# Linear attention and a gated feed-forward layer on one core: the sums over keys in two column halves of the TensorE array

## The chip, the cores and the metric

The kernel runs on one core of one Trainium2 chip. A core has TensorE (PE, matrix products), VectorE (DVE), ScalarE (ACT), GpSimd (POOL) and SyncE (SP, which issues the DMAs here). The metric is the device time of one execution in microseconds (us). A product on PE has a stationary operand, which is loaded into the array first (a weight load, PEld in the profile), and a moving operand, which is streamed through it; the result goes to partitions of a PSUM bank, one partition for each stationary column.

## The reference

For 8 batches and 8 heads of 576 tokens with 64 numbers each, attention is computed with feature maps in place of a softmax. The output of all heads then goes through a gated feed-forward layer (4608 tokens, 512 to 1536 to 512).

```python
def phi(x):
    proj = np.einsum('bhsd,df->bhsf', x, w_phi)          # 64 -> 128
    proj = proj - np.max(np.abs(proj), axis=-1, keepdims=True)
    return np.concatenate([np.exp(proj), np.exp(-proj)], axis=-1)   # 256 features
q_p, k_p = (phi(q), phi(k))
kv = np.einsum('bhsf,bhsd->bhfd', k_p, v)
z = np.sum(k_p, axis=2)
num = np.einsum('bhsf,bhfd->bhsd', q_p, kv)
den = np.einsum('bhsf,bhf->bhs', q_p, z)[..., None] + 1e-06
x = num / den                      # then, over all tokens and heads:
out = (silu(x @ w_gate) * (x @ w_val)) @ w_out
```

The part in question is `kv` and `z`: sums over the 576 keys of a head.

## The kernel before, in words

Two heads are handled together as a pair; there are 32 pairs. For a pair, the keys come in five tiles of 128 tokens (the last holds the remaining 64 tokens of both heads), in three groups: two tiles, two tiles, and the last one (`GROUPS`). For each group PE projects the keys (128 tokens to 128 features for each head), DVE finds the largest absolute value of each token and head (L449) and subtracts it (L454, the centring), ACT takes the two exponentials (L458, L459), and PE multiplies the 128 features of each sign, as stationary operand, by the values (64 numbers and two ones, so that the sum `z` comes along) as moving operand. These last products are the sums over keys. The function `values` issues them: L474 for the four full tiles, once for each tile, head and sign (16 products of 66 columns in a pair), and L467 for the last tile, once for each sign (2 products of 132 columns, both heads at once). They accumulate in one bank, `ps_kv`, whose 128 partitions are the 128 features. All operands here are float32. When the last tile is in, ACT copies the sums out (L495), and they are the stationary operand of the numerators and denominators of the queries.

The queries of the first 8 pairs are handled as the keys are; for the other 24, their largest values are found with DVE's 32 by 32 transposes (L573), a reduction (`largest`, L581), a merge over groups of partitions (`over_groups`, L584 to L589) and another transpose (L593).

The feed-forward layer runs on tiles of 384 tokens, with each float32 number split in a high and a low part and three products for one; from about 720 us on it runs alone, in another form (`pair`, L1008).

The order on every engine is made when the program is built. Each piece of work is a step with an engine, an estimated cost, a rank and the steps it comes after; a small simulation of the engines (`Plan.run`) starts, on each free engine, the ready step with the lowest rank, and writes the instructions in that order. The sums are one step for each group, with the cost `2 * n * pe32(D2)`. On the chip each engine works through its own list, and semaphores hold it where an operand isn't ready. Where PE has no ready step, the plan puts in a product with zeros (L1092 to L1096).

Of the kernel before, what the change touches and what calls it, by code (L numbers as in the profile page):

```python
# [17 lines left out]
P = 128  # L18
S = 576
# [14 lines left out]
D2 = D + 2  # L34
# [30 lines left out]
class Plan:  # L65
# [16 lines left out]
    def add(self, eng, cost, fn, after=(), rank=0.0, take=None, give=None):  # L82
        s = Step(eng, cost, fn, rank, len(self.steps), self.LAG[eng], take, give, (rank, len(self.steps)))
        seen = set()
        for a in after:
            if a is not None and id(a) not in seen:
                seen.add(id(a))
                a.then.append(s)
                s.left += 1
        s.early = self.early  # L90
        self.steps.append(s)
        return s
# [79 lines left out]
def dve(n):  # L172
    return 150 + 1.04 * n
# [10 lines left out]
def act(n):  # L184
    return 190 + 0.86 * n


def pe(n):
    return max(58, 7 + 0.441 * n)


def pe32(n):
    return 2 * max(112, 0.85 * n)
# [3 lines left out]
def favor_attention_moe(ctx: ExitStack, tc: tile.TileContext, qT, kT, v, w_phi, wg, wv, wo, out):  # L197
    nc = tc.nc
# [44 lines left out]
    def view(tag, shape, dtype=F32, when=0, o=None):  # L243
        n = size(shape)
        if o is None:
            o = filled.get((tag, when), 0)
            filled[tag, when] = o + n
        assert o + n <= ROOM[tag], (tag, when, o + n)
        made = lambda: shaped(space(tag, when, F32 if dtype is U32 else dtype)[:, o:o + n], shape, dtype)
        return made if when else made()  # L250

    get = lambda x: x() if callable(x) else x
# [6 lines left out]
    vf = [view("m2", [5, 2, D2])] * 2  # L259
# [16 lines left out]
    def bank(name):  # L276
        return banks.tile([P, 512], F32, name=name, tag=name)
# [3 lines left out]
    ps_kv = bank("kv")  # L281
# [26 lines left out]
    add = plan.add  # L308

    def matmuls(terms):  # L310

        for o, l, r, a, z in terms:
            nc.tensor.matmul(o, l, r, start=a, stop=z)  # L313
# [56 lines left out]
    last = {}  # L370

    def attention(i, rank):
# [4 lines left out]
        one = 0 if early else j  # L377
# [3 lines left out]
        rk, rq, rm, rn, rt = (rank + (0 if early else o) for o in OFFSETS)  # L381
# [22 lines left out]
        n = 4 * P * P  # L404
# [19 lines left out]
        for g, (t0, t1) in enumerate(GROUPS):  # L424

            tail = t1 == 5
            w = t1 - t0
            n = 1 if tail else 2 * w
            key = ("k", i, g)
            buf = (3 * i + g) % 2  # L430
            view = lambda key=key, n=n: work[plan.bank[key]][:, :n * NF].rearrange("p (n f) -> p n f", f=NF)
            room = kp[buf].rearrange("p t h s f -> p (t h) s f")[:, :n]

            def project(t0=t0, t1=t1, key=key, tail=tail):
                o = work[plan.bank[key]]
                for t in range(t0, t1):
                    c = slice(t * P, (t + 1) * P)
                    acc = o[:, :NF] if tail else o[:, (t - t0) * 256:(t - t0 + 1) * 256]
                    if plain:
                        matmuls([(acc, get(kin[one])[:, c], wst if tail else wbd, True, True)])  # L440
                    else:
                        khi, klo = (ks()[:, n, c] for n in range(2))
                        w_hi, w_lo = (wst_hi, wst_lo) if tail else (wbd_hi, wbd_lo)
                        matmuls([(acc, khi, w_hi, True, False), (acc, khi, w_lo, False, False), (acc, klo, w_hi, False, True)])

            width = NF if tail else 256
            kproj = add("PE", w * (pe32(width) if plain else 3 * pe(width)), project, k_ready, rk, take=key)
            m = km[(3 * i + g) % len(km)][:, :n]
            kmax = add("DVE", dve(n * NF), lambda m=m, view=view: vec.tensor_reduce(  # L449
                out=m, in_=view(), axis=AX.X, op=ALU.max, apply_absolute_value=True),  # L450
                       [kproj, last.get(("km", 3 * i + g - 4))], freeing)

            def centre(n=n, m=m, view=view, room=room):
                vec.tensor_tensor(out=room[:, :, 1], in0=view(), op=ALU.subtract,  # L454
                                  in1=m.rearrange("p (n o) -> p n o", o=1).broadcast_to([P, n, NF]))

            ksub = add("DVE", dve(n * NF), centre, [kmax, last.get(("kp", 3 * i + g - 2))], freeing, give=key)
            e0 = add("ACT", act(n * NF), lambda x=room: nc.scalar.activation(x[:, :, 0], x[:, :, 1], AF.Exp), [ksub], rk)  # L458
            e1 = add("ACT", act(n * NF), lambda x=room: nc.scalar.activation(x[:, :, 1], x[:, :, 1], AF.Exp, scale=-1.0),  # L459
                     [e0], rk)  # L460
            last["km", 3 * i + g] = ksub

            def values(t0=t0, t1=t1, room=room, tail=tail):
                kv_open[0] = not tail
                if tail:
                    for k in range(2):
                        nc.tensor.matmul(ps_kv[:, 2 * k * D2:2 * (k + 1) * D2], room[:, 0, k],  # L467
                                         get(vf[one])[:, 4].rearrange("p h d -> p (h d)"), start=False, stop=k == 1)
                    return
                for t in range(t0, t1):  # L470
                    for h in range(2):
                        for k in range(2):
                            o = ps_kv[:, (2 * k + h) * D2:(2 * k + h + 1) * D2]
                            nc.tensor.matmul(o, room[:, 2 * (t - t0) + h, k], get(vf[one])[:, t, h], start=t + h + k == 0, stop=False)  # L474

            kv = add("PE", 2 * n * pe32(D2), values, [e1, *v_in, last.get(("kv", i - 1)), *kv_steps[-1:]], rk)
            last["kp", 3 * i + g] = kv
            kv_steps.append(kv)
# [22 lines left out]
        if early:  # L501
            for g, (t0, t1) in enumerate(GROUPS):
                tail = t1 == 5
# [3 lines left out]
                n = 3 * i + g  # L507
                key, key2 = ("q", i, g), ("t", i, g)
                m, y = km[n % len(km)], qy[n % 2]
                view = lambda key=key, u=u: work[plan.bank[key]][:, :u * NF].rearrange("p (t f) -> p t f", f=NF)  # L510

                def project(t0=t0, t1=t1, key=key, tail=tail):
# [7 lines left out]
                mx = add("DVE", dve(u * NF), lambda u=u, m=m, view=view: vec.tensor_reduce(  # L520
                    out=m[:, 4:4 + u], in_=view(), axis=AX.X, op=ALU.max, apply_absolute_value=True),
                    [pj, last.get(("qm", n - len(km)))], rank)
# [26 lines left out]
        else:  # L549
            copies, q_lo = [], []  # L550
            for h in range(2):
# [6 lines left out]
                for part in range(2):  # L558
# [3 lines left out]
                    def project(h=h, c=c, key=key):  # L562
# [10 lines left out]
            turns = [add("DVE", dve(S), lambda h=h: vec.transpose(qe[j][:, h], qx[j][:, h]),  # L573
                         [*copies[2 * h:2 * h + 2], *use("qe")], rm) for h in range(2)]

            per_head = lambda f: [(lambda h=h: f(h)) for h in range(2)]
# [6 lines left out]
            def over_groups():  # L583
# [4 lines left out]
                vec.tensor_copy(qu[32:64], qu[0:32])  # L588
                vec.tensor_copy(qu[64:128], qu[0:64])  # L589

            mx = [add("DVE", dve(S), f, [turns[h]], rm) for h, f in enumerate(per_head(largest))]
            mg = add("DVE", 6 * 170, over_groups, [*mx, last.get(("back", i - 1))], rm)
            back = [add("DVE", dve(S), f, [mg], rm) for f in per_head(lambda h: vec.transpose(  # L593
                blocks(qe[j], h), qu[:, cols(h)].rearrange("p (a o) -> p a o", o=1).broadcast_to([P, NBL, 32])))]
            last["back", i] = back[1]
# [35 lines left out]
        t0 = add("DVE", dve(S), lambda: vec.transpose(turned, den), [*copied, *done[0], *done[1]], rt)  # L631
# [14 lines left out]
        if held:  # L646
            start, width = held[0][0], sum(w for _, w in held)
# [47 lines left out]
    def low_parts(f, layer, made=None):  # L695

        users = lo_user[layer]
        n = len(users)
        users.append([])
        t = (w1_lo, w2_lo)[layer][n % LO_SETS]  # L700
        if made is not None:
            return users[-1], t, made
        after = [lo_stored[f, a] for a in ((0, 1), (2,))[layer]] + (users[n - LO_SETS] if n >= LO_SETS else [])
        cut = (slice(0, 2 * DM), slice(2 * DM, 3 * DM))[layer]
        flat = t.rearrange("p a k f -> p (a k f)") if layer == 0 else t
        b = n % LO_SETS
        for k in ((2 * b, 2 * b + 1), (2 * LO_SETS + b,))[layer]:
            after += rest_user.get(k, [])
        return users[-1], t, [add("SP", P * (2 - layer) * DM * 4, lambda: nc.sync.dma_start(
            flat.bitcast(F32), wlo_dram[f, :, cut]), after, FIRST)]  # L710
# [111 lines left out]
    def attend(tokens):  # L822
        while made[0] < min(NB * NPAIR, NPAIR * ((tokens + S - 1) // S)):
            attention(made[0], float(made[0]))
            made[0] += 1
# [11 lines left out]
    for f in range(NFT):  # L837
# [3 lines left out]
        for c in range(EARLY):  # L841
            if c == EARLY - 1 and f == NFT - 1:
                put_off()
            j, h = first(c, f, low)
# [12 lines left out]
    for c in range(EARLY, PAIRS):  # L857
        if c == PAIRS - 1:
            attend(NCH * CH)
        for f in range(NFT):  # L860
            j, h = first(c, f, low_parts(f, 0))
# [221 lines left out]
    at, g, ha_, hb_, lo2, tail = waiting.pop()  # L1083
# [64 lines left out]
```

## Time and profile before

| | |
|---|---|
| median of 3 runs | 1263.96 us (1260.27 to 1263.97) |
| the profiled execution | 1263.36 us |
| its span, first to last instruction | 1261.6 us |
| mean granted TensorE clock | 0.997 |
| PE busy | 1240.2 us (98%) |
| PE's weight loads (PEld) | 1145.5 us (91%) |
| DVE busy | 942.8 us (75%) |
| ACT busy | 687.5 us (54%) |
| POOL busy | 241.5 us (19%) |

Sums over keys run in the first 720 us, but for the time from 200 to 300 us, when none do. Weight loads run beside products, so PE and PEld are not added. The end of a product in the trace is modelled, and its time includes its way through the array; how fast products follow one another is read from a run of them. A line of a group names the line of the program, the engine, the operation, what is written and read, the stationary block (`128*128`), the moving block and the count; behind the bar stand the busy time, the mean of one in ns, and idle time ahead of it.

### The profile page before, as it was taken

The numbers are of one execution on the slowest core, as the hardware profiler recorded it, in microseconds if no ns is written. First come the engines' busy times: TensorE is split into PE (matmuls) and PEld (weight loads), VectorE is DVE, ScalarE is ACT, GpSimd is POOL, SyncE is SP. The second block draws the span as 40 slices with busy tenths as digits, with TensorE's granted clock in tenths as the row PEclk, the third lists the DMA queues.
The fourth block names the chain that finished last, engine by engine and source line by source line (L and its number), as shares of the span: only waits on it lengthen the run. The fifth ranks groups of instructions, "written<-read, shape, count | busy, mean of one in ns | idle before, by whom it ended". The sixth has DMA issues, their size and how long they took to land.

```text
span 1261.6 us, 19300 instructions
## 1 busy us (share of the span) xinstructions
PE 1240.2 (98%) x7008; PEld 1145.5 (91%) x7008; DVE 942.8 (75%) x1674; ACT 687.5 (54%) x1419; POOL 241.5 (19%) x306
## 2 busy tenths in 40 slices
PE   9999999999999999999999999989999999999998
PEld 8887999999888998999999999979998999989997
DVE  7997799998899898999989632476557656575553
ACT  5887333336788787777778522233334433353333
POOL 0000000000000000000000010065565655565550
PEclk9999999999999999999999999999999999999999
DMA  4443355557554433343443244542213322222211
GB/s 137 135 116 99 132 176 173 178 167 211 164 153 123 130 92 114 117 121 114 141 118 97 86 152 151 175 150 76 71 55 111 117 73 76 75 101 75 76 51 51
DMA packets 107312, 149.26 MB, mean 118 GB/s; under 512 B 52048, under 2 KB 61776, under 8 KB 107216
## 3 DMA queue, kind: packets, MB, share of 16 engines
q1 hardware_dynamic: 106752, 147.76, 37.7%
q8 instruction: 55, 0.90, 0.3%
q14 instruction: 41, 0.34, 0.1%
q10 hardware_dynamic: 464, 0.26, 0.1%
HBM read 119.67 MB, written 28.31 MB: 117 GB/s over the span
## 4 chain that ended last, share of the span: by engine, by line
PE 89%; DVE 5%; DMA 2%; ACT 1%; POOL 1%; issue 1%; SPq 0%; DVEq 0%; ACTq 0%; POOLq 0%
PE gv L313 23%; PE gv L1008 19%; PE o L313 19%; PE work L313 17%; PE kv L474 8%; PE kv L313 2%; PE kv L467 1%; POOL a L915 1%; POOL a L920 1%; DVE m L953 0%; DVE xl L957 0%; PE o L536 0%; DMA x_dram<-m 0%; DVE m L525 0%; DMA out_dram<-osb 0%
## 5 line engine op out<-in xcount | busy, mean ns | idle before, releaser
L313 PE MATMUL gv<-xh,w_hi 128*128 128x384 f32 x576 | 200.6, 348 | 1.4 <-DVE th L744 1.4
L313 PE MATMUL gv<-xh,w_lo 128*128 128x384 f32 x576 | 193.3, 336 | 0.0
L313 PE MATMUL gv<-xl,w_hi 128*128 128x384 f32 x576 | 193.3, 336 | 0.0
L1008 PE MATMUL gv<-xh,m 128*128 128x384 f32 x504 | 150.6, 337 | 3.1 <-ACT m L1016 2.5
L915 POOL TENSOR_TENSOR a<-w_hi,m 128x256 f32<-128x256 f32 x48 | 40.3, 869 | 500.5 <-DMA m<-wlo_dram 492.7
L915 POOL TENSOR_TENSOR a<-w_hi,w_lo 128x256 f32<-128x256 f32 x96 | 85.7, 922 | 193.6 <-DMA w_lo<-wlo_dram 169.9
L920 POOL TENSOR_TENSOR a<-a 128x256 f32<-128x256 f32 x144 | 114.9, 798 | 8.5
L313 PEld LDWEIGHTS gv<-xh,w_hi 128*128 128x128 f32 x576 | 108.3, 188 | 5.1 <-DVE th L744 2.0
L313 PE MATMUL work<-m,m 128*128 128x288 f32 x408 | 110.2, 408 | 1.7 <-ACT m L624 1.7
L313 PE MATMUL o<-w_hi,hh 128*128 128x512 f32 x270 | 111.3, 412 | 0.0
L313 PEld LDWEIGHTS gv<-xl,w_hi 128*128 128x128 f32 x576 | 108.3, 188 | 3.1 <-DVE xl L659 0.2
L1019 DVE TENSOR_TENSOR a<-gv,a 128x384 f32<-128x384 f32 x72 | 39.9, 554 | 93.9 <-PE gv L1008 93.6
L313 PEld LDWEIGHTS gv<-xh,w_lo 128*128 128x128 f32 x576 | 108.1, 188 | 0.0
L313 PE MATMUL o<-w_hi,hl 128*128 128x512 f32 x270 | 107.2, 397 | 0.0
L1008 PEld LDWEIGHTS gv<-xh,m 128*128 128x128 f32 x504 | 93.2, 188 | 6.0 <-ACT m L1016 3.1
L313 PE MATMUL o<-w_lo,hh 128*128 128x512 f32 x243 | 95.7, 394 | 0.0
L313 PEld LDWEIGHTS work<-m,m 128*128 128x128 f32 x408 | 75.6, 190 | 19.2 <-ACT m L624 2.0
L742 ACT ACTIVATE th<-gv 128x384 f32<-128x384 f32 x72 | 35.3, 490 | 96.5 <-PE gv L313 93.4
L767 ACT CAST hh<-th 128x384 fp32r<-128x384 f32 x108 | 55.2, 511 | 52.5 <-DVE th L747 39.1
L474 PEld LDWEIGHTS kv<-m,m 128*128 128x128 f32 x640 | 75.9, 192 | 3.6 <-ACT m L458 1.2
L1008 PE MATMUL gv<-xh,w_hi 128*128 128x384 f32 x216 | 73.0, 338 | 4.9 <-DVE a L1019 4.9
L474 PE MATMUL kv<-m,m 128*128 128x66 f32 x640 | 75.5, 273 | 1.3 <-ACT m L458 1.0
(183 smaller groups left out, 2993.9 us busy)
## 6 DMA issues: line engine op xcount, KB each, us to landing
w_lo<-wlo_dram SPq DMA_DIRECT2D x60, 512.0 KB, 3.6
w_lo<-wlo_dram SPq DMA_DIRECT2D x78, 256.0 KB, 3.1
wlo_dram<-w_lo SPq DMA_DIRECT2D x36, 256.0 KB, 2.1
out_dram<-osb SPq DMA_DIRECT2D x30, 256.0 KB, 2.9
a<-in_wg_dram SPq DMA_DIRECT2D x12, 512.0 KB, 3.6
a<-in_wv_dram SPq DMA_DIRECT2D x12, 512.0 KB, 3.6
a<-in_wo_dram SPq DMA_DIRECT2D x12, 512.0 KB, 3.7
m<-wlo_dram SPq DMA_DIRECT2D x12, 512.0 KB, 3.5
```

Source lines behind the costliest of these rows:

```text
L313: nc.tensor.matmul(o, l, r, start=a, stop=z)
L467: nc.tensor.matmul(ps_kv[:, 2 * k * D2:2 * (k + 1) * D2], room[:, 0, k], get(vf[one])[:, 4].rearrange("p h d -> p (h d)"), start=False, st ...
L474: nc.tensor.matmul(o, room[:, 2 * (t - t0) + h, k], get(vf[one])[:, t, h], start=t + h + k == 0, stop=False)
L742: s1 = add("ACT", act(CH), lambda: nc.scalar.activation(t_, ps_gv[0][:, :CH], AF.Tanh, scale=0.5), [ends[0], th_free[j]], FIRST)
L767: s4 = add("ACT", act(CH), lambda: nc.scalar.copy(get(hh[b]), th[j]), [made, hid_free[b]], FIRST)
L915: gp.tensor_tensor(out=full()[:, block(n)], in0=hi[:, block(n)], in1=get(low)[:, block(n)], op=ALU.add)
L920: gp.tensor_tensor(out=x[:, block(o)], in0=x[:, block(l)], in1=x[:, block(r)], op=ALU.subtract)
L1008: nc.tensor.matmul(o[:, :CH], l, r, start=begin and i == 0, stop=i == len(terms) - 1, skip_group_check=True)
L1019: return add("DVE", dve(CH), lambda: vec.tensor_tensor(out=snap[n](), in0=bank_c[:, :CH], in1=snap[n](), op=ALU.add), after, FIRST)
```

## The change

Each product of the sums over keys is written as two: one with the first 64 of the 128 stationary columns, which writes partitions 0 to 63 of the bank, and one with the other 64, which writes partitions 64 to 127. The moving operand of both is the same. The branch for the last tile is folded into the loop, and its two products become four in the same way. The plan's cost of the step stays as it was. A dependency is added: on the 24 later pairs, the search for the largest values (`largest`) comes after the merge (`over_groups`) of the pair before, which uses the same small tiles.

```diff
             def values(t0=t0, t1=t1, room=room, tail=tail):
                 kv_open[0] = not tail
-                if tail:
-                    for k in range(2):
-                        nc.tensor.matmul(ps_kv[:, 2 * k * D2:2 * (k + 1) * D2], room[:, 0, k],
-                                         get(vf[one])[:, 4].rearrange("p h d -> p (h d)"), start=False, stop=k == 1)
-                    return
                 for t in range(t0, t1):
-                    for h in range(2):
+                    for h in range(1 if tail else 2):
                         for k in range(2):
-                            o = ps_kv[:, (2 * k + h) * D2:(2 * k + h + 1) * D2]
-                            nc.tensor.matmul(o, room[:, 2 * (t - t0) + h, k], get(vf[one])[:, t, h], start=t + h + k == 0, stop=False)
+                            x = room[:, 2 * (t - t0) + h, k]
+                            y = get(vf[one])[:, 4].rearrange("p h d -> p (h d)") if tail else get(vf[one])[:, t, h]
+                            n = (2 * k + h) * D2
+                            for r in (slice(0, P // 2), slice(P // 2, P)):
+                                nc.tensor.matmul(ps_kv[r, n:n + (2 if tail else 1) * D2], x[:, r], y,
+                                                 start=t + h + k == 0, stop=tail and k == 1)
...
-            mx = [add("DVE", dve(S), f, [turns[h]], rm) for h, f in enumerate(per_head(largest))]
+            mx = [add("DVE", dve(S), f, [turns[h], last.get(("mg", i - 1))], rm) for h, f in enumerate(per_head(largest))]
             mg = add("DVE", 6 * 170, over_groups, [*mx, last.get(("back", i - 1))], rm)
+            last["mg", i] = mg
```

The order on each engine stays the same, but for the doubled rows. Two places on PE show it. The first is the start of the program, in the first pair, before and after; `wbd` and `wst` are the projection's weights, `ident` is for the transposes of the queries:

```order
L313 MATMUL work_133<-wst,m_0_105 128x128
L474 MATMUL kv<-m_0_105,m_0_104 128x66 x8
L536 MATMUL o_127<-ident,m_0_105 128x128 x4
L474 MATMUL kv<-m_0_105,m_0_104 128x66 x8
L467 MATMUL kv<-m_0_105,m_0_104 128x132 x2
L536 MATMUL o_128<-ident,m_0_105 128x128 x4
```

```order
L313 MATMUL work_133<-wst,m_0_105 128x128
L472 MATMUL kv<-m_0_105,m_0_104 64x66 x16
L535 MATMUL o_127<-ident,m_0_105 128x128 x4
L472 MATMUL kv<-m_0_105,m_0_104 64x66 x16
L472 MATMUL kv<-m_0_105,m_0_104 64x132 x4
L535 MATMUL o_128<-ident,m_0_105 128x128 x4
```

The runs of sums stand where they stood, with twice the products of half as many partitions.

The second is a later pair, between products of the feed-forward layer (`gv`, L313) and the projections of queries (`wst_hi`, `wst_lo`), before and after:

```order
L313 MATMUL gv_129<-xl_101,w_hi_77 128x384
L313 MATMUL gv_129<-xh_98,w_lo_95 128x384
L474 MATMUL kv<-m_0_105,m_0_104 128x66 x16
L467 MATMUL kv<-m_0_105,m_0_104 128x132 x2
L313 MATMUL work_132<-a_1_2452,wst_hi 128x288
```

```order
L313 MATMUL gv_129<-xl_101,w_hi_77 128x384
L313 MATMUL gv_129<-xh_98,w_lo_95 128x384
L472 MATMUL kv<-m_0_105,m_0_104 64x66 x32
L472 MATMUL kv<-m_0_105,m_0_104 64x132 x4
L313 MATMUL work_132<-a_1_2614,wst_hi 128x288
```

Here too only the sums' rows differ, and on either side of them stand products with 128 stationary columns (the number in `a_1_2614` is a tile's running number).

## The prediction

> **What bounds the kernel now.** First the page's engine table and its slices, then the chain of waits.
>
> ```profile
> PE 1240.2 (98%) x7008; PEld 1145.5 (91%) x7008; DVE 942.8 (75%) x1674; ACT 687.5 (54%) x1419; POOL 241.5 (19%) x306
> PE   9999999999999999999999999989999999999998
> DVE  7997799998899898999989632476557656575553
> PE 89%; DVE 5%; DMA 2%; ACT 1%; POOL 1%; issue 1%; SPq 0%; DVEq 0%; ACTq 0%; POOLq 0%
> PE gv L313 23%; PE gv L1008 19%; PE o L313 19%; PE work L313 17%; PE kv L474 8%; PE kv L313 2%; PE kv L467 1%; POOL a L915 1%; POOL a L920 1%; DVE m L953 0%; DVE xl L957 0%; PE o L536 0%; DMA x_dram<-m 0%; DVE m L525 0%; DMA out_dram<-osb 0%
> ```
>
> TensorE (PE) is busy for 98% of the 1261.6 us and carries 89% of the chain. The sums over keys, L474 and L467, are 9% of the chain, about 114 us. That is what the change can touch. But where these sums run (the first 23 of 40 slices), VectorE (DVE) is also at 7 to 9 tenths. So I took the windows in which they run, first for all engines.
>
> ```profile
> 0.00:100.00 100.00, 97.27 (x598) 87.86 (x599) 87.66 (x171) 74.32 (x171) 1.34 (x13) 0.98 0.45 128
> 100.00:200.00 100.00, 95.72 (x545) 89.47 (x545) 83.56 (x162) 45.53 (x94) 0.00 (x0) 1.00 0.44 144
> 300.00:400.00 100.00, 100.00 (x582) 87.48 (x582) 87.45 (x169) 78.54 (x173) 0.00 (x0) 1.00 0.53 158
> 400.00:500.00 100.00, 98.02 (x601) 89.38 (x600) 89.21 (x173) 77.24 (x169) 0.00 (x0) 1.00 0.40 113
> 500.00:600.00 100.00, 100.00 (x644) 93.22 (x643) 93.57 (x173) 77.80 (x169) 0.00 (x0) 1.00 0.39 117
> 600.00:720.00 120.00, 120.00 (x758) 111.15 (x757) 105.61 (x204) 88.29 (x193) 0.00 (x0) 1.00 0.37 110
> ```
>
> The columns are PE, its weight loads, DVE, ACT. The same windows for the instructions of L474 alone, PE and its loads:
>
> ```profile
> 0.00:100.00 100.00, 26.91 (x224) 26.75 (x224) 0.98 0.45 128
> 100.00:200.00 100.00, 7.58 (x64) 7.46 (x64) 1.00 0.44 144
> 300.00:400.00 100.00, 18.84 (x160) 19.26 (x160) 1.00 0.53 158
> 400.00:500.00 100.00, 18.62 (x160) 18.93 (x160) 1.00 0.40 113
> 500.00:600.00 100.00, 22.42 (x192) 22.66 (x192) 1.00 0.39 117
> 600.00:720.00 120.00, 26.32 (x224) 26.80 (x224) 1.00 0.37 110
> ```
>
> From 300 to 720 us PE is busy 418 of 420 us and DVE 375.8 of 420. PE is the bound there, but DVE stands close behind: it has 44 us of idle time in that stretch. 736 of the 1024 L474 products lie there, 288 before 200 us. What DVE waits for from 300 to 720 us:
>
> ```profile
> DVE m L631 <- ACT m L624: 11.0, 8, 4.7
> DVE m L573 <- ACT m L568: 6.6, 9, 1.1
> DVE km L449 <- PE work L313: 5.1, 13, 1.0
> DVE th L747 <- PE gv L313: 4.6, 6, 2.8
> DVE th L744 <- ACT th L742: 2.1, 1, 2.1
> DVE hl L768 <- ACT hh L767: 1.1, 4, 0.4
> DVE a L419 <- ACT a L417: 0.3, 1, 0.3
> ```
>
> These add up to 30.8 us; the rest of the 44 are gaps between instructions that no faster PE closes. So from 300 to 720 us at most 30.8 us can be won, whatever PE saves.
>
> **What one product costs.** The groups of the sums:
>
> ```profile
> L474 PEld LDWEIGHTS kv<-m,m 128*128 128x128 f32 x640 | 75.9, 192 | 3.6 <-ACT m L458 1.2 <-ACT m L459 0.6
> L474 PE MATMUL kv<-m,m 128*128 128x66 f32 x640 | 75.5, 273 | 1.3 <-ACT m L458 1.0 <-ACT m L459 0.2
> L474 PE MATMUL kv<-a,m 128*128 128x66 f32 x384 | 45.2, 272 | 0.0
> L467 PE MATMUL kv<-m,m 128*128 128x132 f32 x80 | 13.2, 289 | 0.0
> L467 PE MATMUL kv<-a,m 128*128 128x132 f32 x48 | 7.7, 284 | 0.0
> ```
>
> Two pieces of the chain in order of time (start, length), where products follow one another:
>
> ```profile
> 412.56 3.52 PE kv L474 x32
> 401.52 1.94 PE work L313 x8
> ```
>
> And PE's timeline, the products of the second piece, a running row of sums, and a row that starts after a wait:
>
> ```profile
> 401.35 2.10 PE L313 MATMUL work<-m,m 128*128 128x288 f32 x8
> 9.14 1.91 PE L474 MATMUL kv<-m,m 128*128 128x66 f32 x16
> 12.50 0.44 PE L474 MATMUL kv<-m,m 128*128 128x66 f32 x2 [1.00 <-ACT m L458]
> ```
>
> The 273 ns mean of one includes its way through the array; in a row they follow each other every 3.52/32 = 0.110 us. The program writes 32 x 16 = 512 such products and the trace has 640 + 384 = 1024: each float32 product is two passes, each with its own weight load. The tails are 64 written, 128 in the trace. A float32 product of 288 columns takes 1.94/8 = 0.242 us, or 0.84 ns a column, with its load hidden. At that rate 66 columns need 0.055 us. The pass takes 0.110, twice that, so what paces it is the load of 128 stationary columns, 0.110 us. The 132 columns of a tail stream in 0.111 us, level with their load.
>
> **The change, part by part.** Every engine keeps its order of instructions; each sums product becomes two with 64 stationary columns, so 512 + 64 written products become 1024 + 128, and 1152 pairs of load and pass become 2304. No DMA is added or moved.
>
> *Rate of the pairs.* No row shows a load of fewer than 128 columns. Upper bound: a half load costs the whole 0.110 us and halves follow one another: 4 x 0.110 where 2 x 0.110 stood, +0.22 us for each of 576 written products, +127 us. Middle: a half load costs half, 0.055, and halves follow one another: 4 x 0.055 = 0.22, no change. Lower bound: the loads and passes of the two halves also run side by side, each half paced by 2 x 0.055 (load and stream equal): 0.11 instead of 0.22, for 512 products -56 us. The tails win nothing even so, as their stream alone needs 2 x 0.111. I take side by side, at 0.12 for imperfect starts: -0.10 x 512 = **-51 us of PE time**. The nearest row is the 288-column one, where a load runs wholly under a stream on the same columns; two halves of the columns share even less. The Trainium skill, TensorEngine Tiling (Array Packing), Key Properties, says that tiles work independently and may load and multiply in parallel; by it the sum is this lower bound, and no run here shows it yet.
>
> *Borders.* All other products keep 128 columns, so PE passes between 64 and 128 stationary columns at each end of each run of sums. In PE's order there are 70 such runs, so 140 borders. No row of before shows a border. Lower bound 0. Upper bound a full stop and restart: after the wait at 12.50 us two products took 0.44 us, where two in a running row take 2 x 0.110; that is 0.22 us more, 31 us for 140. I take half, 0.11: **+15 us**. The same section of the Trainium skill says that changing the tiling mode drains the array; by it the sum would go by 31 instead of 15, and no row here can tell.
>
> *What reaches the end.* PE saves 51 - 15 = 36 us: 26 of them from 300 to 720 us (736/1024), 10 before 200. In the later stretch only 30.8 us of DVE's idle time can vanish. A faster run of sums brings the next evictions and centrings forward, but DVE is 88 to 94% taken, and the orders are fixed, so some of the time comes back as PE waiting for DVE. I take a little over half: 14 of 26, and likewise 6 of 10. After 720 us no sums run. **Sum: -20 us.** From the profiled execution's own 1263.36 us (span 1261.6 plus 1.8 around it) that is 1243; from the median of 1263.96, **1244 us**.
>
> *Costed at nothing.* The new dependency of the largest-per-group step (L581) on the merge of the pair before orders two steps on DVE that already stood in that order. Eight of the centrings (L454) also get a wait on ACT's exponentials, which read that buffer two groups earlier; the products that follow those exponentials were waited for already. If that cover were gone, DVE's next reduction and, behind it, the next projection would be late by one exponential. Weight bytes read are the same.
>
> **The rivals.**
> - *Borders decide.* The halves follow one another (no gain) and each border is a full stop: 140 x 0.22 = +31 us, all of it on PE, which is the bound there: 1295; at half the price 1279. For: PE has no slack to hide a stop. Against: nothing in before shows that the array must empty. Without side by side, it is slower by over 0.3% (3.8 us, about what a measurement can tell from no change) once a border costs more than 3.8/140 = 0.03 us. Chance 0.28, from 1268 to 1295.
> - *It does not do what it says.* The halves take turns at half price and borders are free: 4 x 0.055 against 2 x 0.110, 1264, from 1260 to 1268. For: loads and passes start in one stream of instructions, and no row shows PE starting load and pass pairs steadily closer than 0.110 us. Chance 0.15.
> - *A half load costs a whole one.* +127 us, 1391. For: no row with fewer columns. Against: the load's 0.110 us looks like 128 columns of one each 0.86 ns, much as the stream's 0.84. The Trainium skill, TensorE: Matmul & The Clock Gate, Part 3, has loads overlap running products only where the row groups differ; both halves use all rows, so by it load and pass of 0.055 each would come one after another, 4 x 0.11, the same price; the 288-column row speaks against it. Chance 0.04.
>
> **How the numbers follow.** Forecast, side by side with some cost at the borders: 0.53. Its own range: at best borders are free, all 30.8 us of DVE's waits go and half of the 56 x 288/1024 = 16 us before 200 us, 1264 - 39 = 1225; at worst 31 us of borders leave PE 51 - 31 = 20, of which a third is seen, 1257. The range over cases, **1228 to 1288**, leaves out a little at the bottom, the dearest third of the border case and the 1391. Faster: 0.52 (the forecast but for its edge); same: 0.15 (the halves taking turns); slower: 0.33 (borders, whole loads).
>
> **What would show it.** The group of products with 64 columns should have 2048 + 256 members with their loads at twice the number; a run of 64 (32 before) in the chain should last near 2.0 us where 3.5 stood. If it lasts 3.5, the halves take turns; 7 us, a half load is a whole one. PE's idle time, and the first product after each run, show the borders: starts late by 0.1 to 0.2 us. In the windows from 300 to 720 us DVE's share should rise towards 95% and PE's waits on DVE or ACT appear. The forecast is wrong if the runs do not shorten, or if they shorten and DVE's idle time stays while PE waits for it.

## The result, and the profile after

The changed kernel takes 1244.63 us (median of 4 runs, 1243.28 to 1246.74); the kernel before, run beside it, 1262.9 us. The ratio is 0.9861, with a 95% interval of 0.9847 to 0.9876: 18 us faster. The profiled execution took 1244.83 us with a span of 1243.0. The forecast was 1244.

The page of the changed kernel, its engines, its slices and the chain's shares:

```profile
PE 1215.6 (98%) x8160; PEld 1087.3 (87%) x8160; DVE 940.5 (76%) x1674; ACT 686.3 (55%) x1419; POOL 241.8 (19%) x306
PE   8999999999999999999999999989999999999998
DVE  7998799998899899999999632575658655675553
PE 84%; DVE 9%; DMA 3%; ACT 2%; POOL 1%; issue 1%; SPq 0%; DVEq 0%; ACTq 0%; POOLq 0%
PE gv L313 22%; PE gv L1008 19%; PE o L313 19%; PE work L313 16%; PE kv L472 5%; PE kv L313 2%; DVE m L454 1%; DVE km L449 1%; POOL a L915 1%; POOL a L920 1%; DMA w_lo<-wlo_dram 1%; DVE xl L957 1%; DVE m L953 1%; DVE m L593 0%; DVE m L633 0%
```

The sums were 9% of the chain and are 5%. PE has 1152 more instructions and 25 us less busy time. DVE's part of the chain grew from 5% to 9%: the chain now leaves PE more often. Where the time went shows in the first and last start of the sums that read the later values, in the kernel before and (second fence) in the changed one:

```profile
L474 PE MATMUL kv<-a,m x384: 218/275/276, 313.0 to 716.3; 128*128 128x66 f32 x192
```

```profile
L472 PE MATMUL kv<-a,m x864: 219/222/327, 309.8 to 698.3; 128*64 128x66 f32 x154, 128*64 128x132 f32 x19
L472 PEld LDWEIGHTS kv<-a,m x864: 132/137/139, 309.8 to 698.2; 128*64 128x64 f32 x173
```

The changed kernel is 3.2 us ahead when these begin and 18.0 us when they end. After them nothing more is won: all of the difference is made where the sums run.

How much a run of sums shrank is seen in PE's timeline. The kernel before, a run of 16 passes with the products around it:

```profile
432.08 0.40 PE L313 MATMUL o<-w_hi,hl 128*128 128x512 f32 x1
432.32 1.89 PE L474 MATMUL kv<-a,m 128*128 128x66 f32 x16
434.02 0.38 PE L313 MATMUL work<-a,wst_hi 128*128 128x288 f32 x1
```

The same run in the changed kernel, now 32 passes:

```profile
424.95 0.40 PE L313 MATMUL o<-w_hi,hl 128*128 128x512 f32 x1
425.28 1.16 PE L472 MATMUL kv<-a,m 128*64 128x66 f32 x32
426.37 0.40 PE L313 MATMUL work<-a,wst_hi 128*128 128x288 f32 x1
```

From the start of the product ahead to the start of the product behind it was 434.02 - 432.08 = 1.94 us and is 426.37 - 424.95 = 1.42 us. Two pieces of the chain of the changed kernel (start, length) give the rate without the ends:

```profile
425.35 1.08 PE kv L472 x32
442.78 2.02 PE kv L472 x64
```

The second 32 passes cost 0.94 us, so a product as it was written before (8 in 32 passes) costs 0.1175 us, where 0.224 stood (the pieces of 32 and 16 passes before lasted 3.52 and 1.73 us: 1.79/8). That is 0.106 less for each of 512, **54.5 us** of PE time. But the run of 16 above would then have shrunk by 8 x 0.106 = 0.85 us and shrank by 0.52. The rest sits at its two ends: the first pass of the run begins 0.33 us after the product ahead of it, where it was 0.24, and the product behind follows later too.

### The profile page after: what moved, and what is told of

It reads as the page before. It is cut to its first block, busy times and chain, and to the rows that moved or that the text cites. A ratio compares the mean times of both kernels' runs of the same rounds, so it can differ in the third digit from the quotient of the medians.

```text
span 1243.0 us, 21611 instructions
## 1 busy us (share of the span) xinstructions
PE 1215.6 (98%) x8160; PEld 1087.3 (87%) x8160; DVE 940.5 (76%) x1674; ACT 686.3 (55%) x1419; POOL 241.8 (19%) x306
## 4 chain that ended last, share of the span: by engine, by line
PE 84%; DVE 9%; DMA 3%; ACT 2%; POOL 1%; issue 1%; SPq 0%; DVEq 0%; ACTq 0%; POOLq 0%
PE gv L313 22%; PE gv L1008 19%; PE o L313 19%; PE work L313 16%; PE kv L472 5%; PE kv L313 2%; DVE m L454 1%; DVE km L449 1%; POOL a L915 1%; POOL a L920 1%; DMA w_lo<-wlo_dram 1%; DVE xl L957 1%; DVE m L953 1%; DVE m L593 0%; DVE m L633 0%
## 5 line engine op out<-in xcount | busy, mean ns | idle before, releaser
L313 PE MATMUL gv<-xh,w_hi 128*128 128x384 f32 x576 | 200.6, 348 | 2.4 <-DVE th L744 1.4
L313 PE MATMUL gv<-xh,w_lo 128*128 128x384 f32 x576 | 193.3, 336 | 0.0
L313 PE MATMUL gv<-xl,w_hi 128*128 128x384 f32 x576 | 193.2, 335 | 0.0
L313 PEld LDWEIGHTS gv<-xh,w_hi 128*128 128x128 f32 x576 | 108.3, 188 | 6.7 <-DVE th L744 2.0
L313 PE MATMUL work<-m,m 128*128 128x288 f32 x408 | 110.6, 408 | 0.7 <-ACT m L624 0.7
L313 PE MATMUL o<-w_hi,hh 128*128 128x512 f32 x270 | 111.1, 411 | 0.0
L313 PEld LDWEIGHTS gv<-xl,w_hi 128*128 128x128 f32 x576 | 108.3, 188 | 3.1 <-DVE xl L659 0.2
L313 PEld LDWEIGHTS gv<-xh,w_lo 128*128 128x128 f32 x576 | 108.1, 188 | 0.0
L313 PE MATMUL o<-w_hi,hl 128*128 128x512 f32 x270 | 106.7, 395 | 0.0
L313 PE MATMUL o<-w_lo,hh 128*128 128x512 f32 x243 | 95.6, 393 | 0.0
L313 PEld LDWEIGHTS work<-m,m 128*128 128x128 f32 x408 | 75.5, 189 | 19.0 <-ACT m L624 1.0
L744 DVE SCALAR_TENSOR_TENSOR th<-th,gv 128x384 f32<-128x384 f32 x72 | 39.5, 548 | 46.1 <-ACT th L742 45.5
L768 DVE TENSOR_TENSOR hl<-th,hh 128x384 fp32r<-128x384 f32 x108 | 66.5, 618 | 8.7 <-ACT hh L767 8.4
```

What stands on the lines that cost most here:

```text
L744: s2 = add("DVE", dve(CH), lambda: nc.vector.scalar_tensor_tensor(out=t_, in0=t_, scalar=1.0, in1=ps_gv[0][:, :CH], op0=ALU.add, op1=ALU.m ...
L768: s5 = add("DVE", dve(CH), lambda: nc.vector.tensor_tensor(out=get(hl[b]), in0=th[j], in1=get(hh[b]), op=ALU.subtract), [s4], FIRST)
```

## The experiments

All comparisons are with the kernel before, run on the same chip; ratios are given with their 95% interval. The changed kernel stands at 0.9861.

Each execution also has a mean granted TensorE clock, and the time follows it: on the chip of the runs with less VectorE and less ScalarE work, the kernel before took 1260.77 us at a clock of 1.000, 1263.18 to 1264.79 at 0.997 and 1266.65 at 0.994, about 1 us for each thousandth. The changed kernel's four runs had 0.997 to 1.000, some experiments had less. So where a few microseconds matter, runs at equal clocks are compared too. Seen like that the changed kernel is 17 to 18 us ahead (1243.28 against 1260.77 at 1.000; 1244.83 against 1261.96 and 1263.02 at 0.998).

**The halves one after another.** The same products, borders and counts, in an order in which neighbours use the same half of the columns.

```diff
-                for t in range(t0, t1):
-                    for h in range(1 if tail else 2):
-                        for k in range(2):
...
-                            for r in (slice(0, P // 2), slice(P // 2, P)):
+                for r in (slice(0, P // 2), slice(P // 2, P)):
+                    for t in range(t0, t1):
+                        for h in range(1 if tail else 2):
+                            for k in range(2):
```

> The changed kernel, but each step issues all its products for the first 64 columns and then all for the other 64, so that neighbours in the row use the same half. Same count of loads, passes and borders. Theory A (the halves run side by side, which needs neighbours on different halves; borders cost about 0.16 us each): a run of 32 passes takes about 32 x 0.058 = 1.8 us in place of 1.08, as long as a run of 16 before; the 140 borders remain and nothing pays for them: 22 us slower than before, 1285 us, range 1272 to 1300. Rival B (a half load and pass is simply cheap, whichever half its neighbour uses): the run stays near 1.1 us and the time near 1245 us.

Measured: 1277.24 us, ratio 1.0115 (1.0092 to 1.0138), slower than before by 13.5 us. The same run in its timeline, and then two of its groups, whose busy time was 48.2 and 45.1 us in the changed kernel:

```profile
437.80 0.40 PE L313 MATMUL o<-w_hi,hl 128*128 128x512 f32 x1
438.13 1.91 PE L472 MATMUL kv<-a,m 128*64 128x66 f32 x32
439.96 0.40 PE L313 MATMUL work<-a,wst_hi 128*128 128x288 f32 x1
```

```profile
L472 PEld LDWEIGHTS kv<-m,m 128*64 128x64 f32 x1440 | 76.7, 137 | 14.8 <-issue 7.8 <-ACT m L458 1.7 <-ACT a L335 1.3
L472 PE MATMUL kv<-m,m 128*64 128x66 f32 x1280 | 73.6, 225 | 1.2 <-ACT m L458 0.8 <-ACT m L459 0.3
```

The run takes 2.16 us, 0.74 more than in the changed kernel and 0.22 more than before. So the gain hangs on neighbours in different halves, and theory A holds: a half load and pass alone costs half a whole one (single passes follow each other every 0.058 us in the trace), which wins nothing, and only side by side does it pay. The time is at the low end of the range, since where the run passes from the first half to the second a few passes still run in pairs.

**What a border costs.** A product of zeros with 128 stationary columns between the two tiles of each full step, in the kernel before (it costs its own load) and in the changed one (it makes two more borders as well).

```diff
                 for t in range(t0, t1):
+                    if t == t0 + 1:
+                        nc.tensor.matmul(ps_kv[:, 4 * D2:4 * D2 + P], nil, nil, start=False, stop=False)
```

> The kernel before, with one product of zeros (128 stationary and 128 moving columns, to a part of the bank that nothing reads) between the two tiles of each of the 64 full steps. Theory A: each costs its own load, 0.11 us, 7 us in all on TensorE, which is the bound: 1270 us (1266 to 1274). Rival (a switch between float32 and the other product form costs something by itself): more than 0.2 us each, 1277 us or more.

> The changed kernel with the same product of zeros between the two tiles of each of the 64 full steps, so that each run of halves is cut in two and 128 borders are added. Theory A (0.16 us a border): each cut costs 0.11 + 0.32 = 0.43 us, 27 us on TensorE; some is taken out of its slack, so 1261 to 1272 us, 1266. Rival (the array must empty, 0.22 a border or more): 0.55 us a cut, 1272 to 1282 us. Rival (borders are free and the runs lose their time elsewhere): 0.11 a cut, 1250 us.

Measured: 1269.26 us, 1.0041 (1.0028 to 1.0054), and 1258.94 us, 0.9964 (0.9950 to 0.9978). The cut run, first in the kernel before with zeros, then in the changed one with zeros:

```profile
435.89 0.40 PE L313 MATMUL o<-w_hi,hl 128*128 128x512 f32 x1
436.12 1.00 PE L476 MATMUL kv<-a,m 128*128 128x66 f32 x8
436.93 0.31 PE L472 MATMUL kv<-nil 128*128 128x128 f32 x1
437.07 1.05 PE L476 MATMUL kv<-a,m 128*128 128x66 f32 x8
437.93 0.38 PE L313 MATMUL work<-a,wst_hi 128*128 128x288 f32 x1
```

```profile
429.94 0.40 PE L313 MATMUL o<-w_hi,hl 128*128 128x512 f32 x1
430.27 0.69 PE L474 MATMUL kv<-a,m 128*64 128x66 f32 x16
430.88 0.33 PE L467 MATMUL kv<-nil 128*128 128x128 f32 x1
431.14 0.69 PE L474 MATMUL kv<-a,m 128*64 128x66 f32 x16
431.76 0.40 PE L313 MATMUL work<-a,wst_hi 128*128 128x288 f32 x1
```

The cut costs 2.04 - 1.94 = 0.10 us in the one and 1.82 - 1.42 = 0.40 us in the other. The difference of 0.30 is two borders: **0.15 us a border**, 21 us for 140. So a border isn't free. The second time, 1259, is lower than A expected for another reason: at 0.40 us the 64 cuts would add 26 us; the stretches of PE that hold sums, from the start of the product ahead to the start of the product behind, grew by 20 us in all 70 runs (114.8 to 134.7), and the time by 14. That the rest went into waits that PE had already is likely, but not shown; what PE waits for is the next question.

**The last tile whole.**

```diff
-                            for r in (slice(0, P // 2), slice(P // 2, P)):
+                            for r in ((slice(0, P),) if tail else (slice(0, P // 2), slice(P // 2, P))):
```

> The changed kernel, but the products of the last tile keep 128 stationary columns. Theory A: these gain nothing from halves, since their 132 columns stream as long as the load, and where such a step stands alone (17 of 32) it pays two borders for nothing, 0.31 us each, 5 us of TensorE; a little over half reaches the end: 1242 us (1239 to 1244). Rival (tails gain as the others do): 64 x 0.1 = 6 us more TensorE time, 1248 us.

Measured: 1246.71 us (1241.55 to 1247.44), 0.9857 (0.9833 to 0.9882): no difference from the changed kernel that can be told. In the trace, the stretches of PE that hold sums add up to 140.9 us before, 114.8 in the changed kernel and 110.0 here. So the last tiles do cost 4.8 us in halves and gain nothing, as A said. That the time does not show it has a reason in the clock: these four runs had only 0.993 to 0.998. At equal clocks they are 19 to 21 us ahead of the kernel before (1246.44 against 1266.19 at 0.994; 1241.55 against 1261.96 and 1263.02 at 0.998), so some 2 to 3 us of the 4.8 reach the end, near A's little over half.

**Three eighths of the sums left out (192 of 512 products), without any halves.**

```diff
                     for h in range(2):
-                        for k in range(2):
+                        for k in range(2 if t == 0 else 1):
```

> The kernel before (128 columns, no borders), with the products of the negative sign left out for tiles 2 to 4 of each pair: 192 of 512 products, 384 passes of 0.110 us, 42 us less of TensorE time; the sums are incomplete. Theory A (VectorE stands close behind TensorE in this part, so only a little over half of what TensorE saves is seen): 24 us faster, 1239 us (1232 to 1247). Rival (TensorE alone is the bound, and the changed kernel saved only some 18 us on it): all 42, 1221 us.

Measured: 1246.45 us, 0.9866 (0.9842 to 0.9890). Of 42 us of PE work taken away, 18 are seen, and about 21 at an equal clock (1245.16 and 1245.51 against 1266.94, all at 0.994); A had 24, and there are no borders here to blame. The stretches with sums shrank by 31.2 us (140.9 to 109.7), of which about two thirds are seen, as in the changed kernel (18 of 26.1). So where the sums run, PE's saving does not reach the end whole, whichever way it is made.

**Is it VectorE's work, or ScalarE's?** First the transposes that spread the largest values, cut from 18 blocks to 2, in both kernels.

```diff
-                blocks(qe[j], h), qu[:, cols(h)].rearrange("p (a o) -> p a o", o=1).broadcast_to([P, NBL, 32])))]
+                blocks(qe[j], h)[:, :2], qu[:, cols(h)].rearrange("p (a o) -> p a o", o=1)[:, :2].broadcast_to([P, 2, 32])))]
```

> The kernel before, with the 48 transposes that spread the largest values back (0.76 us each) cut from 18 blocks to 2, so about 0.6 us less each, some 29 us less of VectorE time between 200 and 720 us; the centring of the queries is incomplete. Theory A: TensorE is the bound there, VectorE close behind: 4 to 10 us faster, 1256 us. Rival (VectorE is not in the way at all): within 2 us, 1262 us.

> The changed kernel with the same shorter transposes; the centring of the queries is incomplete. Theory A (what TensorE saved and does not show is waiting for VectorE): it gains more than the kernel before does, 10 to 18 us, 1231 us. Rival (the rest of the saving was eaten on TensorE by borders): the same gain as before has, 4 us or less more than it.

Measured: before 1263.67 us, 1.0007 (0.9989 to 1.0025), nothing; after 1243.09 us, 0.9837 (0.9813 to 0.9861), 1.5 us by the medians and 0.24% by the ratios. At equal clocks the second is 20 to 22 us ahead of the kernel before (1241.07 against 1261.50 and 1261.95 at 0.998), so 3 to 4 us better than the changed kernel. That is the direction of theory A, which expected 10 to 18 us. Then much more, from the changed kernel, on each engine:

```diff
-vec.transpose(qe[j][:, h], qx[j][:, h])
+vec.transpose(qe[j][:, h, :64], qx[j][:, h, :64])
...
-in_=blocks(qe[j], h), axis=AX.X
+in_=blocks(qe[j], h)[:, :, :8], axis=AX.X
...
-out=qx[j][:, h], in0=qx[j][:, h], in1=qe[j][:, h], op=ALU.subtract
+out=qx[j][:, h, :64], in0=qx[j][:, h, :64], in1=qe[j][:, h, :64], op=ALU.subtract
...
-qe[j][:, h], qx[j][:, h], AF.Exp
+qe[j][:, h, :SH // 2], qx[j][:, h, :SH // 2], AF.Exp
```

(The first three pairs and the shorter transpose are the one kernel, the last pair and its twin with the negative sign the other.)

> The changed kernel, with VectorE's work on the later queries cut much further: the turn, the turn back and the subtraction on 64 of 576 columns, the search for the largest on 8 of 32 numbers, about 110 us less of VectorE time between 200 and 720 us; the queries' centring is mostly left out. Theory A2 (of the 26 us that the sums gave up on TensorE some 8 went into waits of TensorE for VectorE's results, which come late since VectorE works through its list): most of these waits go, 1236 us (1232 to 1239). Rival B2 (they wait for ScalarE, which empties the banks and takes the exponentials): within 3 us of the changed kernel, 1244 us.

> The changed kernel, with the two exponentials of the later queries on 144 of 576 columns, about 35 us less of ScalarE time between 200 and 720 us; the features of the other columns are wrong. Theory A2: within 2 us of the changed kernel, 1244 us. Rival B2 (TensorE's new waits are for ScalarE): 1237 us (1233 to 1240).

Measured: with less VectorE work 1243.27 us, 0.9831 (0.9815 to 0.9846); with less ScalarE work 1245.27 us, 0.9852 (0.9839 to 0.9865). Both expectations of a gain of 7 us or more fell. But with less VectorE work the clock was 0.994 to 1.000, and at equal clocks that kernel is 21 to 23 us ahead of the kernel before (1239.48 against 1260.77 at 1.000, 1244.49 against 1266.65 at 0.994), 4 to 5 us better than the changed kernel. With less ScalarE work it is 15 to 18 us (1245.89 against 1260.49 and 1262.70 at 0.999), no gain. From 300 to 720 us in the changed kernel, then with less VectorE work, then with less ScalarE work (columns as in the windows above):

```profile
300.00:720.00 420.00, 415.18 (x3487) 354.75 (x3486) 379.39 (x725) 326.12 (x713) 0.00 (x0) 1.00 0.43 128
```

```profile
300.00:720.00 420.00, 416.39 (x3506) 358.52 (x3505) 290.93 (x728) 328.11 (x717) 0.00 (x0) 1.00 0.45 131
```

```profile
300.00:720.00 420.00, 414.39 (x3486) 354.83 (x3485) 379.10 (x725) 297.67 (x715) 0.00 (x0) 1.00 0.44 128
```

VectorE has 88 us less to do in this stretch and ScalarE 28 us less, and PE gets through 19 passes more, or one fewer. The same from the first to the last start of the later sums: the kernel before, the changed one, less VectorE work, less ScalarE work:

```profile
313.00:716.30 403.30, 401.32 (x2490) 366.56 (x2488) 363.07 (x691) 311.90 (x680) 0.00 (x0) 1.00 0.41 121
309.80:698.30 388.50, 383.68 (x3323) 326.84 (x3324) 360.69 (x691) 310.34 (x680) 0.00 (x0) 1.00 0.43 126
311.90:696.40 384.50, 380.89 (x3323) 327.13 (x3324) 275.09 (x694) 310.26 (x680) 0.00 (x0) 1.00 0.44 127
311.80:700.30 388.50, 382.89 (x3325) 327.09 (x3324) 360.58 (x691) 282.65 (x680) 0.00 (x0) 1.00 0.44 126
```

With VectorE relieved of some 86 us, the same passes take 4.0 us less (384.5 after 388.5); with ScalarE relieved, exactly as long. So VectorE's work holds PE for some 4 us there, ScalarE's amount of work not at all. How much the kernel before would win by the larger cut was not measured; by the shorter transposes it won nothing.

**A plan that knows the new cost.**

```diff
-            kv = add("PE", 2 * n * pe32(D2), values, ...
+            kv = add("PE", n * pe32(D2) + 330, values, ...
```

> The changed kernel, with the plan told what a step of sums now costs (224 ns for each written product and 330 ns for the two borders, where 448 stood), so the order on the engines is planned anew. Theory A (the old order keeps some of TensorE's saving from showing): 3 to 8 us faster than the changed kernel, 1239 us. Rival (the orders are no limit, VectorE's own work is): within 2 us of it, 1245 us.

(For one of the 512 written products the plan's cost goes from 224 to 112 ns by this edit; the 448 and 224 of the expectation are for two of them.)

Measured: 1268.84 us, 1.0043 (1.0026 to 1.0059), 24 us slower than the changed kernel. The first and last start of its sums, then the window from 800 us on, then PE's longest wait there:

```profile
L472 PEld LDWEIGHTS kv<-a,m x864: 132/137/139, 315.7 to 792.1; 128*64 128x64 f32 x173
```

```profile
800.00:840.00 40.00, 23.14 (x91) 19.64 (x90) 24.89 (x26) 14.00 (x24) 20.04 (x18) 0.74 0.47 153
```

```profile
PE gv L1008 <- ACT xh L956: 13.8, 2, 9.0
```

The planned attention ends at 792 us where it ended at 698, and PE stands still for 17 of the 40 us behind it, waiting for the first operands of the last stage (L956). The rates of the sums are those of the changed kernel (a run of 32 passes takes 1.08 us). What changed in the program is the order alone. In that window the granted clock was 0.74 (the third figure from the end), and in all ten runs the mean was 0.983 to 0.989; against 0.997 to 1.000, at about 1 us a thousandth, that goes with about 12 of the 24 us (an estimate). Whether the standstill brings the clock down is not shown. Both theories fell: the order matters, but not in this direction.

**The second group and the last tile in one step**, so that no last tile stands alone; then the same with the new cost.

```diff
+            held.append(values)
+            if g == 1:
+                continue
...
-            kv = add("PE", 2 * n * pe32(D2), values, ...
+            kv = add("PE", 2 * (5 if tail else n) * pe32(D2), run, ...
```

(`run` calls the held functions in turn.)

> The changed kernel, but the sums of the second group and of the last tile are one step, so that no run holds a last tile alone; the plan is made anew for it. Borders at 0.15 us: 17 runs of last tiles lose their borders, 5 us less TensorE time; the second group's sums wait for the last tile's exponentials. If TensorE's savings show: 1241 us. If they go into waits as they did with whole last tiles: 1244 us or a little more.

> The same joined step, with the plan told the new cost of the sums (224 ns a written product and 330 ns for the borders). The earlier run with the new cost alone was 24 us slower than the changed kernel, since the planned attention then ran past 720 us and left TensorE waiting there. If the new cost by itself does that: again 1260 us or more. If it was an accident of that order: near 1243 us.

Measured: joined 1241.4 us (1239.21 to 1245.07), 0.9828 (0.9813 to 0.9842); joined with the new cost 1266.71 us, 1.0017 (1.0006 to 1.0027). The first is about 3 us better than the changed kernel, and its interval does not touch that kernel's (22 us ahead of the kernel before at equal clocks, 1239.21 against 1260.49 and 1262.70 at 0.999); of the kernels that leave nothing out it is the fastest. This is what was expected if PE's savings show. The second again loses what the new cost loses, again at a low clock (0.982 to 0.989 in all twelve runs), so that was no accident of one order.

## Why the prediction was right, point by point

- **What bounds it: right.** PE does. What was added to it landed: halves in turn, +12.7 us in the stretches with sums (140.9 to 153.7), +13.5 in the time.
- **Rate, side by side at 0.12 us a product: right.** 0.1175 measured; 54.5 us of PE time where 51 were forecast, and a run of 64 passes in 2.02 us where "near 2.0" was to show it. The two halves' passes start 6 to 7 ns apart in the trace, one pair every 0.058 us. The bound chosen by the nearest row, a load hidden under a stream, was the right one. The Trainium skill, TensorEngine Tiling (Array Packing), Key Properties, said that tiles load and multiply in parallel; the trace agrees, with 0.224/0.1175 = 1.9 times the rate.
- **Half a load costs half: right**, shown by the halves in turn. The rival at 1391 us is gone. The Trainium skill, TensorE: Matmul & The Clock Gate, Part 3, has loads overlap running products only where the row groups differ; the trace does not agree: both halves use all 128 rows, and their loads start 6 to 7 ns apart and run beside the other half's passes.
- **Last tiles win nothing: right**; they lose 4.8 us on PE.
- **Borders: the kind of cost right, the size a third too small, and its nearness luck.** 0.11 us was taken as half of a full restart, 0.15 was measured; 21 us where 15 stood. The restart itself was misread. The 0.44 us of the two passes at 12.50 us reach to the end of the second and so include its way through the array, 0.27 us, which the 0.110 between neighbours leaves out; the row of 16 at 9.14 us has that, too (1.91, where 16 x 0.110 is 1.76), without any stop. Two passes in a running row take 0.11 + 0.27 = 0.38 in the same measure, so the restart costs about 0.06 us and not 0.22, and a border costs more than that. Half of a figure that was too large came out near a cost that no row had shown. The rival in which borders decide had the right kind of cost, and would have been near the truth without the side by side: that is the run with halves in turn, 13.5 us slower. The Trainium skill, TensorEngine Tiling (Array Packing), Key Properties, says that changing the tiling mode drains the array; the 0.15 us fit that, but what a border consists of is not shown.
- **What PE saves: less than the sum.** By the prices it is 54.5 - 21 = 33.5 us, where the prediction had 36. Measured, the 70 stretches with sums shrank by 140.9 - 114.8 = 26.1 us. The other 7 were lost inside these stretches; the waits of the sums' first loads for exponentials (L458 and L459 below) lie there.
- **What reaches the end: the number right, the reason in part.** 18 us, where 20 were forecast; 14.8 from 300 us on (14 forecast) and 3.2 before (6). But that is 18 of 26.1, over two thirds, and not a little over half of 36: too much saved and too little let through cancel in the sum, which is luck. The prediction put the loss on VectorE's being nearly full ("at most 30.8 us can be won", "some of the time comes back as PE waiting for DVE"). DVE's share did rise, if not towards 95%: from 90.0% to 92.8% between the first and the last of the later sums (363.07 of 403.3, 360.69 of 388.5). And taking 86 us of its work away there gave back 4 us, 4 to 5 in the time at equal clocks: about half of the 8 that were missing. Taking work off ScalarE gave nothing. For the rest the prediction's reason does not hold.
- **Costed at nothing: right.** Among the waits of DVE in the changed kernel, from 300 to 720 us, there is none of the centring (L454) or of the search for the largest values.

What stands beside it: PE's loads now wait, mostly a fraction of a microsecond at a time, for single results. PE's loads (PEld) from 300 to 720 us, in the kernel before (all rows) and then in the changed one (the first seven; line, what was waited for, us in total, times, longest):

```profile
PEld work L313 <- ACT m L624: 2.6, 2, 2.0
```

```profile
PEld kv L472 <- issue: 6.2, 20, 0.4
PEld work L313 <- ACT m L624: 4.3, 7, 1.9
PEld kv L472 <- ACT m L458: 3.5, 10, 0.6
PEld work L313 <- DVE a L554: 3.1, 7, 0.8
PEld kv L472 <- ACT m L624: 1.9, 5, 0.4
PEld kv L472 <- ACT m L459: 1.8, 7, 0.4
PEld work L313 <- DVE m L454: 1.7, 5, 0.6
```

The first row of the second fence is the borders: the first load of a run waits some 0.3 us for nothing that the trace names. The others are a bank not yet emptied (L624), exponentials of the very keys that are to be summed (L458, L459), a low part (L554), a centring (L454). Before, there was one such row. A reading that fits: the work that PE has before it needs such a result is fixed by the planned order; when the sums become shorter, that cover shrinks, and the result comes as late as ever. With less VectorE work the L554 row falls to 1.2 us and the row of L454 is gone, while those of ScalarE's results fall little or stay:

```profile
PEld kv L472 <- ACT m L458: 3.4, 10, 0.6
PEld work L313 <- ACT m L624: 3.2, 2, 1.8
PEld work L313 <- DVE a L554: 1.2, 4, 0.5
```

That these waits are new is shown by the table. How much of each holds PE up is not: the loads' waits from 300 to 720 us add up to 28 us, while PE itself was idle for only 4.8 of the 388.5 us of the later sums (2.0 of 403.3 before). That their cause is the order and the length of each step, for the part that VectorE's load does not explain, is what is left after the two experiments; it is not shown directly. No experiment gave an order that lets everything through: the joined step came 3 us further (4 to 5 at equal clocks), and the two plans with the new cost went the other way. That stays open.

## What to carry to other kernels

Where a float32 product with a short moving operand is paced by its load of 128 stationary columns, splitting the columns in halves, issued in alternation, nearly doubles its rate here (0.224 to 0.1175 us a product); the same halves issued in turn gain nothing. Each passage between whole and half columns costs some 0.15 us here, so keep the runs long: a run of 8 written products won 0.85 us and paid 0.30, and a product whose stream is as long as its load only pays. And on an engine that is 98% busy in a fixed order, part of what is saved comes back as waits for results that were covered before: here 8 of 26 us. How much of that another engine's load explains, its share of busy time leaves open; taking work off it showed it, about half. And before a difference of a few microseconds is read, look at the clocks of the runs: here a thousandth of the clock was 1 us, enough to hide 4.

## What was not expected of the hardware

Two loads into different halves of the columns run side by side, though both read all 128 partitions: a pair of 64-column loads with their passes takes 0.058 us, as long as a single one with halves in turn. A border has a price, and it is paid on both sides: the first pass of a run starts about 0.09 us later than it did (0.33 after the product ahead, where 0.24 stood), and the rest falls on the second pass and on the product behind.
